# Attention scores in tiles of 32 queries instead of 64, and a split of the last activation and the last results over engines

## The chip, the cores and the metric

The kernel runs on one core of a Trainium2 chip. What counts is the time of one execution on the device, in microseconds (us); a kernel's time is the median of its runs. The core has a matrix engine (TensorE, PE in the profile, whose weight loads stand apart as PEld), VectorE (DVE), ScalarE (ACT), GpSimd (POOL) and SyncE (SP), which issues most of the transfers. Each works through its own list of instructions in order, and semaphores make one wait for another.

## The reference

The first stage is attention over 4 batches, 8 heads, 768 positions and a head width of 64, in which a query sees the keys at distance 0 to 127 behind it and the first 4 keys of the sequence (sinks). The second stage takes the 3072 x 512 result through a two-layer network with an activation of its own.

```
scores = scale * np.matmul(q, k.transpose(0, 1, 3, 2))
keep = (pos[None, :] < n_sink) | ((rel >= 0) & (rel < window))     # rel = query position - key position
a = softmax(np.where(keep, scores, -1e9));  attn = np.matmul(a, v)
x = attn with the 8 heads side by side, 3072 x 512
h = x @ w_in                                                       # 512 x 2048
sp = np.maximum(h, 0.0) + np.log1p(np.exp(-np.abs(h)))
out = (h * erf(sp)) @ w_out                                        # 2048 x 512
```

## The kernel before

**Attention.** It goes in 48 steps. A step `s` is a block of 256 queries (`g`, 12 blocks, 3 in each batch) for one pair of heads (`c`, 4 pairs). `score` (line 387) makes the scores of a step. The two heads of the pair, `h`, lie in the two halves of 64 partitions of the operand `kq` and write to two banks of PSUM, the halves of the tile `both` (`ps` in the profile). The 256 queries are two blocks `i` of 128. For each of them and each head there are two matmuls with 64 queries as the stationary operand: queries 0 to 63 (`lo`) against 208 keys, and queries 64 to 127 (`hi`) against 224 keys, which end in the 16 columns of the sinks. The blocks at the start of a batch (`gb == 0`) have no keys behind their first 128 queries, and there both matmuls of `i = 0` take 144. So a step has 8 matmuls, and since they are in plain float32, each shows as two records on PE: 16 records `L419`, over four quarters of the array (two halves of its rows by two halves of its columns).

A query needs only 128 of those keys. The kernel stores the scores of one query row by key position modulo 128: VectorE copies the wanted part of the overhanging columns onto the unwanted part with `copy_predicated` (line 432, the fold), under the mask `tri`. It takes two calls, one for the partitions of `lo` and one for those of `hi`. Then come the mask and the row minimum (L437), the exponential on ScalarE (L441), the sums and scaling (`norm`), a transpose (`ptrans`, through DRAM from step 15 on), the copies of halves on GpSimd (`phalf`, L528 and L537), and the product with the values (`av`, L579).

**Network.** `hidden` (L784, L788) multiplies a block with 128 columns of `w_in`, `act` (line 793) works out the activation of two such pieces at once, and `project` (L833 to L835) multiplies it with `w_out`. From block 2 on the operands are split into a high part and a low part in float32r: VectorE casts the high part `gh` (L817) and GpSimd subtracts to get the low part `gl` (L818). L833 and L834 need `gh`, and L835 needs `gl`. After the 16th piece of a block, `result` copies its two accumulators of 128 x 512 out of PSUM on ScalarE (L839, tile `ot`), and SyncE writes each to DRAM (L750).

**What sets the order.** The loop over `m` near line 730 emits for each sixteenth of a block its hidden matmuls, the attention work that `plan` puts there, the projections and the activation. `at(a, what)` gives each a priority, and the framework's scheduler makes each engine's final order from priorities and its own model of durations. The model's times are in that order, so an instruction of another size can move its neighbours.

Of the kernel before, what the change touches and what calls it, by code (L numbers as in the profile page):

```python
# [8 lines left out]
F32 = mybir.dt.float32  # L9
# [4 lines left out]
ALU = mybir.AluOpType  # L14
# [4 lines left out]
P = 128  # L19
# [23 lines left out]
DT = 12  # L43

TT = 15

NSINK = 22

# [2 lines left out]
FH = 8  # L51
# [5 lines left out]
UB = 4  # L57
# [4 lines left out]
def kernel(  # L62
# [11 lines left out]
    nc = tc.nc  # L74
    B, H, S, D = q.shape
    NT, DM = out.shape
# [3 lines left out]
    NF = DF // P  # L80
    GT = 256
    GPB = S // GT
    NG = B * GPB
    NU = 4
    NSTEP = NG * NPAIR
    KB, S3 = P + SW, 6 * SW
# [53 lines left out]
    def fast_path():  # L140
        with ExitStack() as st:
# [45 lines left out]
            set_mask(mask0)  # L187
            set_mask(mask1)

            tri = pers.tile([P, 192], mybir.dt.int8, name="tri")[:, :64]  # L190
            nc.vector.tensor_scalar(tri[:64], rf[:64, :64], float(P), None, op0=ALU.is_ge)
            nc.vector.tensor_scalar(tri[64:], rf[64:, 64:128], float(P), None, op0=ALU.is_lt)

# [10 lines left out]
            xp, early = {}, {}  # L206

            stp = {}
            mark = {}
            first, turn = [], []  # L210

            HP = P // 2
# [170 lines left out]
            def score(s, prev):  # L383

                g, c = divmod(s, NPAIR)
                gb = g % GPB
                d = stp[s]
                d["sum"] = small.tile([P, 2, 2], F32, tag="sum", name=f"sum_{s}")
                d["neg"] = small.tile([P, 2, 2], F32, tag="neg", name=f"neg_{s}")

                ps, both = [], None
                for h in range(2):
                    nm = f"ps_{s}_{h}"
                    if s == 1:
                        ps.append(ps_h.tile([P, 2, GT], F32, tag="h", name=nm).rearrange("p a t -> p (a t)"))
                    elif s == 2:
                        ps.append(ps_o.tile([P, DM], F32, tag="o", name=nm))
                    else:
                        if both is None:
                            both = ps_s.tile([P, 2, 512], F32, tag="s", name=f"ps_{s}")  # L400
                        ps.append(both[:, h, :])


                dx = KB + 80
                X = [80, 80 + dx]
                warm(ps[0][:, X[1] : X[1] + P], 3 if s == 0 else 0)
                for i in range(2):
                    qt = kq[:, c, 3 + i, :]
                    kt = kq[:, c].rearrange("p n t -> p (n t)")
                    runs = ((lo, KB * i, KB + 64, X[i]), (hi, KB * i + 64, KB + 80, X[i] - 80))  # L410
                    if gb + i == 0:
                        runs = ((lo, KB, KB, X[i]), (hi, KB, KB, X[i]))
                    for hf, r0, n, x in runs:
                        for h in (1, 0):
                            r = slice(64 * h, 64 * h + 64)
                            with at(pos(s), "rest") if s >= TT + AL else nullcontext():
                                prev = follow(
                                    prev,
                                    nc.tensor.matmul(ps[h][hf, x : x + n], qt[r, hf], kt[r, r0 : r0 + n], start=True, stop=True),  # L419
                                )  # L420

                i0 = int(gb == 0)
                for hf, x, y in ((lo, X[0], X[0] + KB), (hi, X[0] + 64, X[0] - 80)):
                    for t in (both,) if both is not None else ps:
                        t = t if both is not None else t.rearrange("p (h t) -> p h t", h=1)
                        n = t.shape[1]
                        o, w = (
                            t[hf, :, z : z + 2 * dx].rearrange("p h (i t) -> p h i t", i=2)[:, :, i0:, e : e + 64]
                            for z, e in ((min(x, 64), x - min(x, 64)), (min(y, 64), y - min(y, 64)))
                        )  # L430
                        mk = tri[hf].rearrange("p (a b t) -> p a b t", a=1, b=1).broadcast_to([64, n, 2 - i0, 64])
                        nc.vector.copy_predicated(o, mk, w)
                for i in range(2):
                    mk = mask if gb > 0 else (mask0, mask1)[i]
                    for h in range(2):
                        y = pst[:, s % RING, i, h, :]
                        mark["t", s] = nc.vector.tensor_tensor_reduce(  # L437
                            out=y, in0=ps[h][:, X[i] : X[i] + KB], in1=mk, scale=-scale, scalar=3.0e38, op0=ALU.add, op1=ALU.min,
                            accum_out=d["neg"][:, i, h : h + 1],
                        )  # L440
                        mark["e", s] = nc.scalar.activation(  # L441
                            y, y, AF.Exp, bias=d["neg"][:, i, h : h + 1], scale=-1.0, accum_out=d["sum"][:, i, h : h + 1]
                        )
# [268 lines left out]
            gs = {}  # L712
# [17 lines left out]
            for m in range(-LEAD, NG * NF + LAG + 2):  # L730
                a = m + LEAD
                live = 0 <= m < NG * NF
                if live:
                    g, f = divmod(m, NF)
                    if f % 2 == 0:
                        hp = mlp.hid_tile(m)
                    if f > 0:
                        with at(a, "hid"):
                            ahead = mlp.hidden(hp, xp[g], f)
                attn(a)  # L740
                w = m - LAG
                if 0 <= w < NG * NF:
                    g2, f2 = divmod(w, NF)
                    with at(a, "proj"):
                        mlp.project(gs[w // 2], g2, f2, lambda ins: follow(ahead if live and f and g >= 2 else None, ins))
                    if f2 == NF - 1:
                        for i in range(2):
                            r0 = (g2 * 2 + i) * P
                            with at(a, "res"):
                                nc.sync.dma_start(out[r0 : r0 + P, :], mlp.result(g2, i))  # L750
                if live:
                    if f == 0:
                        with at(a, "hid"):
                            mlp.hidden(hp, xp[g], f)
                    if f % 2 == 1:
                        with at(a, "act"):
                            gs[m // 2] = mlp.act(hp, m, m < NF + FH)

                while wn < 32 and a >= 1 and (wn < (0, 0, 3, 5)[a - 1] if a < 5 else wn < 2 * a - 4 or need(order[wn]) <= m + W1):
                    with at(a, "wc"):  # L760
                        wconv(order[wn], wn)
                    wn += 1
                    with at(a, "wl"):
                        for n in order[wl : wn + WQ]:
                            wload(n)
                            wl += 1
                for n in split.get(m, ()):
                    with at(a, "ws"):
                        wsplit(n, m)

    class make_mlp:
# [18 lines left out]
                )  # L790
            return last

        def act(self, hp, m, whole=False):
            work = self.work
            h = hp.rearrange("p a t -> p (a t)")
            r = work.tile([P, 512], F32, tag="r", bufs=1, name=f"r_{m}")
            if whole:
                acc = work.tile([P, 2, 512], F32, tag="g", bufs=2, name=f"gf_{m}")[:, 0, :]
            else:
                acc = None  # L800
            nc.scalar.activation(r, h, AF.Tanh, bias=b_t, scale=0.5)  # L801
            nc.scalar.activation(r, r, AF.Square, bias=b_v, scale=-0.5)  # L802
            nc.scalar.activation(r, r, AF.Square, bias=b_r)  # L803
            for i in range(3):
                u = work.tile([P, 512], F32, tag="u", bufs=UB, name=f"u{i}_{m}")
                sq = nc.scalar.activation(u, r, AF.Square, bias=b_a[i], scale=CS)  # L806
                x = h if i == 0 else acc
                if acc is None:
                    acc = u
                pr = nc.vector.scalar_tensor_tensor(out=acc, in0=u, scalar=CC[i] * CS**2, in1=x, op0=ALU.add, op1=ALU.mult)  # L810
            if isinstance(m, int):
                self.mark[m // 2] = sq, pr
            if whole:
                return (acc,)
            gt = work.tile([P, 2, 512], F32R, tag="g", bufs=2, name=f"g_{m}")
            gh, gl = gt[:, 0, :], gt[:, 1, :]
            nc.vector.tensor_copy(gh, acc)  # L817
            nc.gpsimd.tensor_tensor(gl, acc, gh.bitcast(F32), op=ALU.subtract)  # L818
            return gh, gl

        def project(self, gt, g, f, behind=lambda ins: ins):
# [166 lines left out]
```

## Time and profile before

| | us |
|---|---|
| lowest and highest of three runs | 700.12 and 702.70 |
| median | 701.39 |
| the profiled execution, its own time | 699.65 |
| its span, from the first to the last record | 697.95 |
| PE busy in it | 677.9 |

The profile shows one execution. Its own time stands 1.74 us under the median of the three runs, and 1.7 us of it lie outside the span. Busy times of an engine count a stretch once, even where records overlap. A matmul record lasts longer than the engine needs before it takes the next one, so the price of a matmul on PE is read from the distance between starts, not from the mean duration.

### The profile page before, as it was taken

How to read it: one execution, taken by the hardware profiler on the slowest of the kernel's cores; microseconds unless marked ns; L12 is line 12 of the kernel's file. 1: busy time of each engine (PE TensorE's matmuls, PEld its weight loads, DVE VectorE, ACT ScalarE, POOL GpSimd, SP SyncE). 2: the span in 40 equal slices, each digit the busy share in tenths (PEclk: the TensorE clock that was granted, in tenths of full speed). 3: DMA queues.
4: the chain of work that ended last, by engine and by line, in shares of the span. 5: the costliest groups of instructions: out<-in, count | busy, mean ns of one | idle time of the engine just before them, and what ended most of it. 6: DMA issues, size and time to landing. Idle time of an engine off the chain costs nothing. (4 is left out here: it accounts for less than half of the span.)

```text
span 698.0 us, 16215 instructions
## 1 busy us (share of the span) xinstructions
PE 677.9 (97%) x5550; PEld 565.4 (81%) x5550; DVE 548.2 (79%) x1473; ACT 494.3 (71%) x1157; POOL 305.4 (44%) x501
## 2 busy tenths in 40 slices
PE   8889999999999999999999999999999999999996
PEld 5657656788888788898888898898888898889895
DVE  7999997778889888878698788688689688664352
ACT  4787668987984776686596686687586686686572
POOL 3422371135434564473555444555445444542221
PEclk9999999999999999999999999999999999999999
DMA  7999402103216655543453553553453453320000
GB/s 215 265 320 397 114 16 58 38 16 60 57 36 125 135 118 102 132 92 77 108 111 72 117 96 74 118 115 76 111 103 77 101 106 70 73 49 1 31 2 35
DMA packets 246858, 70.10 MB, mean 100 GB/s; under 512 B 214704, under 2 KB 238896, under 8 KB 246768
## 3 DMA queue, kind: packets, MB, share of 16 engines
q1 hardware_dynamic: 246208, 68.92, 42.2%
q8 instruction: 46, 0.75, 0.5%
q14 instruction: 44, 0.36, 0.2%
q10 hardware_dynamic: 560, 0.07, 0.1%
HBM read 50.27 MB, written 18.42 MB: 98 GB/s over the span
## 5 line engine op out<-in xcount | busy, mean ns | idle before, releaser
L788 PE MATMUL h<-xh,wt 128*128 128x256 f32 x1408 | 268.4, 282 | 1.5 <-DVE gf L810 1.3
L788 PEld LDWEIGHTS h<-xh,wt 128*128 128x128 f32 x1408 | 222.7, 188 | 15.5 <-issue 7.6
L788 PE MATMUL h<-xl,wt 128*128 128x256 f32 x704 | 196.5, 279 | 0.0
L818 POOL TENSOR_TENSOR g<-u,g 128x512 fp32r<-128x512 f32 x84 | 112.6, 1340 | 166.9 <-DVE g L817 151.2
L806 ACT ACTIVATE u<-r 128x512 f32<-128x512 f32 x288 | 162.9, 622 | 18.8 <-DVE gf L810 7.5
L810 DVE SCALAR_TENSOR_TENSOR u<-u,u 128x512 f32<-128x512 f32 x168 | 132.1, 786 | 13.1 <-ACT u L806 0.8
L788 PEld LDWEIGHTS h<-xl,wt 128*128 128x128 f32 x704 | 132.5, 188 | 4.5 <-issue 1.1
L833 PE MATMUL o<-wt,g 128*128 128x512 f32 x336 | 133.0, 396 | 0.8 <-DVE g L817 0.8
L834 PE MATMUL o<-wt,g 128*128 128x512 f32 x336 | 132.0, 393 | 0.0
L835 PE MATMUL o<-wt,g 128*128 128x512 f32 x336 | 130.7, 395 | 0.7 <-POOL g L818 0.5
L441 ACT ACTIVATE pst<-pst,neg 128x144 f32<-128x144 f32 x192 | 77.4, 404 | 64.0 <-DVE neg L437 63.4
L801 ACT ACTIVATE r<-h 128x512 f32<-128x512 f32 x96 | 57.1, 594 | 44.8 <-PE h L788 43.5
L810 DVE SCALAR_TENSOR_TENSOR u<-u,h 128x512 f32<-128x512 f32 x84 | 56.5, 672 | 39.3 <-ACT u L806 36.6
L537 POOL TENSOR_SCALAR_AFFINE_SELECT pz<-pa 64x256 f32<-64x256 f32 (+1 forms) x96 | 57.2, 596 | 55.5 <-ACT pa L499 54.5
L833 PEld LDWEIGHTS o<-wt,g 128*128 128x128 f32 x336 | 63.1, 188 | 14.5 <-ACT u L806 1.7
L835 PEld LDWEIGHTS o<-wt,g 128*128 128x128 f32 x336 | 62.7, 188 | 14.8 <-POOL g L818 1.4
L834 PEld LDWEIGHTS o<-wt,g 128*128 128x128 f32 x336 | 63.1, 188 | 9.7
L817 DVE CAST g<-u 128x512 fp32r<-128x512 f32 x84 | 36.4, 433 | 36.7 <-PE o L835 33.3
L802 ACT ACTIVATE r<-r 128x512 f32<-128x512 f32 x96 | 60.7, 632 | 2.5
L803 ACT ACTIVATE r<-r 128x512 f32<-128x512 f32 x96 | 60.6, 631 | 2.7
L528 POOL COPY pz<-pa 64x256 f32<-64x256 f32 x66 | 29.6, 448 | 66.8 <-DMA pa<-pd 66.0
L419 PE MATMUL ps<-kq 64*64 64x208 f32 (+2 forms) x768 | 49.2, 346 | 0.7 <-ACT kq L372 0.7
(105 smaller groups left out, 921.7 us busy)
## 6 DMA issues: line engine op xcount, KB each, us to landing
pd<-turn SPq DMA_DIRECT2D x33, 320.0 KB, 2.6
pa<-pd SPq DMA_DIRECT2D x132, 80.0 KB, 2.7
ws<-in_moe_w_in_dram SPq DMA_DIRECT2D x16, 512.0 KB, 7.3
ws<-in_moe_w_out_dram SPq DMA_DIRECT2D x16, 512.0 KB, 10.1
out_dram<-ot SPq DMA_DIRECT2D x24, 256.0 KB, 2.1
v<-in_v_dram SPq DMA_DIRECT2D x56, 96.0 KB, 2.5
kq<-in_k_dram SPq DMA_DIRECT2D x144, 32.0 KB, 2.0
kq<-in_q_dram SPq DMA_DIRECT2D x144, 32.0 KB, 2.2
```

What stands on the lines that cost most here:

```text
L441: mark["e", s] = nc.scalar.activation(y, y, AF.Exp, bias=d["neg"][:, i, h : h + 1], scale=-1.0, accum_out=d["sum"][:, i, h : h + 1])
L537: mark["half"] = nc.gpsimd.affine_select(out=out, in_=x, pattern=[[0, 2], [0, 2 - i0], [-sg, HP]], compare_op=op, fill=0.0, base=0, channe ...
L788: last = nc.tensor.matmul(o, wt[NC * j + c][:, p, fs], xt[e][:, c, :], start=(m == 0), stop=(m == len(ops) - 1))
L801: nc.scalar.activation(r, h, AF.Tanh, bias=b_t, scale=0.5)
L802: nc.scalar.activation(r, r, AF.Square, bias=b_v, scale=-0.5)
L803: nc.scalar.activation(r, r, AF.Square, bias=b_r)
L806: sq = nc.scalar.activation(u, r, AF.Square, bias=b_a[i], scale=CS)
L810: pr = nc.vector.scalar_tensor_tensor(out=acc, in0=u, scalar=CC[i] * CS**2, in1=x, op0=ALU.add, op1=ALU.mult)
L818: nc.gpsimd.tensor_tensor(gl, acc, gh.bitcast(F32), op=ALU.subtract)
L833: behind(nc.tensor.matmul(o, gh[:, ws], wt[16 + f][:, 0, :], start=(f == 0), stop=False))
L834: nc.tensor.matmul(o, gh[:, ws], wt[16 + f][:, 1, :], start=False, stop=False)
L835: nc.tensor.matmul(o, gl[:, ws], wt[16 + f][:, 0, :], start=False, stop=(f == NF - 1))
```

## The change

From step 16 on (`SQ = 16`) the scores are made with 32 queries as the stationary operand, so four matmuls stand where two stood, each against 176 keys (144 in the blocks without earlier keys). They write one tile of PSUM that stays allocated from step 16 to the end (`banks["s"]`). At step 16 the widths are 272, 240, 208 and 176, so that every column that is read later has been written once. With the new layout the fold is one call over all 128 partitions and 128 columns, under a mask `tri` of 128 x 128 that is one more instruction at the start; the old one is renamed `tri2`. The low part of the last activation alone is made by VectorE instead of GpSimd. The last two results are each copied in two halves of 256 columns, one by ScalarE and one by VectorE, and each half is written by a transfer of its own, from the queues of ScalarE and SyncE.

```
-            tri = pers.tile([P, 192], mybir.dt.int8, name="tri")[:, :64]
-            nc.vector.tensor_scalar(tri[:64], rf[:64, :64], float(P), None, op0=ALU.is_ge)
-            nc.vector.tensor_scalar(tri[64:], rf[64:, 64:128], float(P), None, op0=ALU.is_lt)
+            tri2 = ... the same two instructions ...
+            tri = pers.tile([P, P], mybir.dt.int8, name="tri")
+            nc.vector.tensor_scalar(tri, rf[:, :P], float(P), None, op0=ALU.is_ge)
...
-                        if both is None:
-                            both = ps_s.tile([P, 2, 512], F32, tag="s", name=f"ps_{s}")
+                        if s <= SQ and both is None:
+                            both = banks["s"] = ps_s.tile([P, 2, 512], F32, tag="s", name=f"ps_{s}")
+                        both = banks["s"]
...
-                X = [80, 80 + dx]
+                X = [0, 240] if s >= SQ else [80, 160 + KB]
...
                     runs = ((lo, KB * i, KB + 64, X[i]), (hi, KB * i + 64, KB + 80, X[i] - 80))
+                    if s >= SQ:
+                        runs = [(slice(j, j + 32), KB * i + j, max(KB + 32, (272 - j) * (s == SQ)), X[i] + j) for j in range(0, P, 32)]
                     if gb + i == 0:
-                        runs = ((lo, KB, KB, X[i]), (hi, KB, KB, X[i]))
+                        runs = [(r[0], KB, KB, X[i]) for r in runs]
...
-                for hf, x, y in ((lo, X[0], X[0] + KB), (hi, X[0] + 64, X[0] - 80)):
+                folds = (... the two of before with tri2 ...) if s < SQ else ((slice(0, P), tri, X[0], X[0] + KB),)
+                for hf, m, x, y in folds:
...
-                                nc.sync.dma_start(out[r0 : r0 + P, :], mlp.result(g2, i))
+                                if w < NG * NF - 1:
+                                    nc.sync.dma_start(out[r0 : r0 + P, :], mlp.result(g2, i))
+                                    continue
+                                acc, hc = mlp.acc.pop((g2, i)), DM // 2
+                                for c0, copy, dma in ((0, nc.scalar.copy, nc.scalar), (hc, nc.vector.tensor_copy, nc.sync)):
+                                    ot = work.tile([P, DM], F32, tag="u", bufs=UB, name=f"ot_{g2}_{i}_{c0}")[:, :hc]
+                                    copy(ot, acc[:, c0 : c0 + hc])
+                                    dma.dma_start(out[r0 : r0 + P, c0 : c0 + hc], ot)
...
-                            gs[m // 2] = mlp.act(hp, m, m < NF + FH)
+                            gs[m // 2] = mlp.act(hp, m, m < NF + FH, nc.vector if m == NG * NF - 1 else nc.gpsimd)
...
-            nc.gpsimd.tensor_tensor(gl, acc, gh.bitcast(F32), op=ALU.subtract)
+            (eng or nc.gpsimd).tensor_tensor(gl, acc, gh.bitcast(F32), op=ALU.subtract)
```

The first place is PE around the scores of step 32, before the change (a row is line, operation, output<-inputs, size of the output, and how many follow each other; `av_30` is the product with the values of step 30, `o_6` an accumulator of block 6).

```order
L579 MATMUL av_30_5523<-pa_30_5270,v_30_5000 64x128 x2
L579 MATMUL av_30_5523<-pa_30_5270,v_30_5000 64x64 x4
L579 MATMUL av_30_5523<-pz_30_5406,vz_131 64x64 x8
L419 MATMUL ps_32_5540<-kq_130 64x208 x2
L419 MATMUL ps_32_5540<-kq_130 64x224 x2
L419 MATMUL ps_32_5540<-kq_130 64x208 x2
L419 MATMUL ps_32_5540<-kq_130 64x224 x2
L833 MATMUL o_6_0_5277<-wt_16_2058,g_97_5131 128x512
```

The same place on PE with the change, where the tile keeps the name of step 16 and the lines have moved down by 7 to 16.

```order
L588 MATMUL av_30_5622<-pa_30_5363,v_30_5087 64x128 x2
L588 MATMUL av_30_5622<-pa_30_5363,v_30_5087 64x64 x4
L588 MATMUL av_30_5622<-pz_30_5505,vz_133 64x64 x8
L426 MATMUL ps_16_2566<-kq_132 32x176 x16
L849 MATMUL o_6_0_5370<-wt_16_2060,g_97_5218 128x512
```

Sixteen matmuls of 176 columns stand between the same neighbours where eight of 208 and 224 stood. Elsewhere from step 16 on the scheduler has also moved hidden matmuls and projections against each other by up to about a dozen places. How often PE goes from one shape of array to another is the same in both orders, 169 times.

The second place is the end of VectorE's list, before the change, with the semaphores that each row waits for (`u0_191` is the last activation, `g_191` its high part).

```order
L817 CAST g_189_9036<-u0_189_9027 128x512 [waits DVE_49,PE_49]
L810 SCALAR_TENSOR_TENSOR u0_191_9080<-u0_191_9080,h_190_9039 128x512 [waits Activation_49]
L810 SCALAR_TENSOR_TENSOR u0_191_9080<-u1_191_9083,u0_191_9080 128x512 [waits DVE_49,Activation_49]
L810 SCALAR_TENSOR_TENSOR u0_191_9080<-u2_191_9086,u0_191_9080 128x512 [waits DVE_49,Activation_49]
L817 CAST g_191_9089<-u0_191_9080 128x512 [waits DVE_49,PE_49]
```

The end of VectorE's list with the change (`o_11_0` and `o_11_1` are the last two accumulators, `ot_11_0_256` the upper half of the copy of the first).

```order
L826 SCALAR_TENSOR_TENSOR u0_191_9275<-u0_191_9275,h_190_9234 128x512 [waits Activation_49]
L826 SCALAR_TENSOR_TENSOR u0_191_9275<-u1_191_9278,u0_191_9275 128x512 [waits DVE_49,Activation_49]
L826 SCALAR_TENSOR_TENSOR u0_191_9275<-u2_191_9281,u0_191_9275 128x512 [waits DVE_49,Activation_49]
L833 CAST g_191_9284<-u0_191_9275 128x512 [waits DVE_49,PE_49]
L834 TENSOR_TENSOR g_191_9284<-u0_191_9275,g_191_9284 128x512 [waits DVE_49]
L765 COPY ot_11_0_256_9314<-o_11_0_8980 128x256 [waits Activation_49]
L765 COPY ot_11_1_256_9320<-o_11_1_8981 128x256 [waits DVE_49,Activation_49]
```

The subtraction has come over from GpSimd, and two half copies stand behind it. Each of them waits for a semaphore of ScalarE (Activation), at the value that ScalarE's own copy of the other half of the same accumulator sets.

The third place is the end of ScalarE's list before the change.

```order
L803 ACTIVATE r_191_9076<-r_191_9076 128x512 [waits Activation_49]
L806 ACTIVATE u0_191_9080<-r_191_9076 128x512 [waits Activation_49,Pool_49]
L806 ACTIVATE u1_191_9083<-r_191_9076 128x512 [waits DVE_49]
L806 ACTIVATE u2_191_9086<-r_191_9076 128x512 [waits DVE_49]
L839 COPY ot_11_0_9116<-o_11_0_8785 128x512 [waits PE_49,Pool_49]
L839 COPY ot_11_1_9119<-o_11_1_8786 128x512 [waits DVE_49,PE_49]
```

The end of ScalarE's list with the change.

```order
L822 ACTIVATE u1_191_9278<-r_191_9271 128x512 [waits DVE_49]
L822 ACTIVATE u2_191_9281<-r_191_9271 128x512 [waits DVE_49]
L765 COPY ot_11_0_0_9311<-o_11_0_8980 128x256 [waits PE_49,Pool_49]
L766 DMA out_0_dram<-ot_11_0_0_9311 128x256 [waits Activation_49]
L765 COPY ot_11_1_0_9317<-o_11_1_8981 128x256 [waits DVE_49,PE_49]
L766 DMA out_0_dram<-ot_11_1_0_9317 128x256 [waits DMAHW3_49,Activation_49]
```

The copies are half as wide, and ScalarE now issues a transfer after each, the first of them ahead of its second copy.

## Rows read from the trace of the kernel before

**Rows 1.** The page's first part: busy us, share, instructions of each engine.
```profile
PE 677.9 (97%) x5550; PEld 565.4 (81%) x5550; DVE 548.2 (79%) x1473; ACT 494.3 (71%) x1157; POOL 305.4 (44%) x501
```
**Rows 2.** Busy time by stretch: from:to, length, PE busy (records), PEclk, DMA share, GB/s.
```profile
206.00:240.00 34.00, 31.79 (x297) 1.00 0.60 122
240.00:640.00 400.00, 399.99 (x3462) 1.00 0.45 93
```
**Rows 3.** PE's waits, 200 to 245 us: waiter <- releaser: us, times, longest.
```profile
PE av L579 <- POOL pa L537: 1.7, 2, 1.6
```
**Rows 4.** PE's timeline around step 32: start, us, line, operands, records [idle before <-releaser].
```profile
398.76 0.99 PE L419 MATMUL ps<-kq 64*64 64x208 f32 x16
399.68 0.51 PE L833 MATMUL o<-wt,g 128*128 128x512 f32 x1
```
**Rows 5.** PE's timeline around step 36, the first of a batch.
```profile
452.04 0.85 PE L419 MATMUL ps<-kq 64*64 64x144 f32 x16
452.82 0.51 PE L833 MATMUL o<-wt,g 128*128 128x512 f32 x1
```
**Rows 6.** PE's timeline of step 32 in three narrow windows: the records then under way.
```profile
398.76 0.41 PE L419 MATMUL ps<-kq 64*64 64x208 f32 x3
...
398.99 0.76 PE L419 MATMUL ps<-kq 64*64 64x208 f32 x12
...
399.17 0.58 PE L419 MATMUL ps<-kq 64*64 64x208 f32 x8
```
**Rows 7.** PE's timeline, 53 to 57 us: float32 matmuls on the whole array.
```profile
53.42 3.94 PE L784 MATMUL h<-xf,wf 128*128 128x256 f32 x17
```
**Rows 8.** VectorE by line and form: count | busy us, mean ns | idle before.
```profile
L432 DVE COPY_PREDICATED ps<-tri,ps 64x256 f32<-64x256 int8 x64 | 27.6, 431 | 3.5 <-PE ps L419 1.2
L702 DVE TENSOR_TENSOR wt<-wf,wt 128x512 fp32r<-128x512 f32 x32 | 21.5, 711 | 0.8 <-ACT wt L701 0.7
L599 DVE TENSOR_TENSOR xl<-av,xh 128x256 fp32r<-128x256 f32 x44 | 18.3, 417 | 9.0 <-ACT xh L598 8.7
L432 DVE COPY_PREDICATED ps<-tri,ps 64x128 f32<-64x128 int8 x28 | 8.3, 297 | 0.9
```
**Rows 9.** VectorE's timeline at the start of the program.
```profile
3.64 0.19 DVE L192 TENSOR_SCALAR tri<-rf 64x64 int8<-64x64 f32 x1
5.03 0.17 DVE L107 CAST tiny<-tiny 128x4 f32<-128x4 int32 x1 [1.20 <-DMA tiny<-in_window_dram]
```
**Rows 10.** The timeline of the end, all engines but PEld.
```profile
688.88 0.43 DVE L817 CAST g<-u 128x512 fp32r<-128x512 f32 x1
...
689.45 1.28 POOL L818 TENSOR_TENSOR g<-u,g 128x512 fp32r<-128x512 f32 x1 [3.61 <-DVE g L817]
...
690.17 0.39 PE L834 MATMUL o<-wt,g 128*128 128x512 f32 x1
690.79 0.74 PE L835 MATMUL o<-wt,g 128*128 128x512 f32 x2 [0.23 <-POOLq L956]
...
692.31 1.22 ACT L839 COPY ot<-o 128x512 f32<-128x512 f32 x2 [4.81 <-PE o L835]
692.92 0.96 SPq L750 DMA_DIRECT2D out_dram<-ot  x2
```
**Rows 11.** ScalarE by line and form.
```profile
L598 ACT CAST xh<-av 128x256 fp32r<-128x256 f32 x44 | 16.0, 365 | 31.2 <-PE av L579 30.8
L839 ACT COPY ot<-o 128x512 f32<-128x512 f32 x24 | 14.1, 586 | 19.2 <-PE o L835 18.4
```
**Rows 12.** A transfer issued on ScalarE's queue, from the timeline of the start.
```profile
1.76 0.49 ACTq L105 DMA_DIRECT2D tiny<-in_window_dram  x1
```

**Rows 13.** Transfers, from the page: operands, queue, count, KB each, median us to landing.
```profile
out_dram<-ot SPq DMA_DIRECT2D x24, 256.0 KB, 2.1
kq<-in_k_dram SPq DMA_DIRECT2D x144, 32.0 KB, 2.0
```
**Rows 14.** The same for the transfers after 690 us.
```profile
out_dram<-ot SPq DMA_DIRECT2D x2, 256.0 KB, 2.3
```

More of the change, by code (lines that the diff above doesn't have):

```diff
@@ L45 @@
 TT = 15
+SQ = 16
 NSINK = 22
@@ L188, in fast_path @@
             set_mask(mask1)
-            tri = pers.tile([P, 192], mybir.dt.int8, name="tri")[:, :64]
-            nc.vector.tensor_scalar(tri[:64], rf[:64, :64], float(P), None, op0=ALU.is_ge)
-            nc.vector.tensor_scalar(tri[64:], rf[64:, 64:128], float(P), None, op0=ALU.is_lt)
+            tri2 = pers.tile([P, 64], mybir.dt.int8, name="tri2")
+            nc.vector.tensor_scalar(tri2[:64], rf[:64, :64], float(P), None, op0=ALU.is_ge)
+            nc.vector.tensor_scalar(tri2[64:], rf[64:, 64:128], float(P), None, op0=ALU.is_lt)
+            tri = pers.tile([P, P], mybir.dt.int8, name="tri")
+            nc.vector.tensor_scalar(tri, rf[:, :P], float(P), None, op0=ALU.is_ge)
             kq = pers.tile([P, NPAIR, 5, KB], F32, name="kq")
@@ L208, in fast_path @@
             stp = {}
-            mark = {}
+            mark, banks = {}, {}
             first, turn = [], []
@@ L398, in score @@
                     else:
-                        if both is None:
-                            both = ps_s.tile([P, 2, 512], F32, tag="s", name=f"ps_{s}")
+                        if s <= SQ and both is None:
+                            both = banks["s"] = ps_s.tile([P, 2, 512], F32, tag="s", name=f"ps_{s}")
+                        both = banks["s"]
                         ps.append(both[:, h, :])
-                dx = KB + 80
-                X = [80, 80 + dx]
+                X = [0, 240] if s >= SQ else [80, 160 + KB]
+                dx = X[1] - X[0]
                 warm(ps[0][:, X[1] : X[1] + P], 3 if s == 0 else 0)
@@ L422, in score @@
                 i0 = int(gb == 0)
-                for hf, x, y in ((lo, X[0], X[0] + KB), (hi, X[0] + 64, X[0] - 80)):
+                folds = ((lo, tri2, X[0], X[0] + KB), (hi, tri2, X[0] + 64, X[0] - 80)) if s < SQ else ((slice(0, P), tri, X[0], X[0] + KB),)
+                for hf, m, x, y in folds:
+                    w = m.shape[-1]
                     for t in (both,) if both is not None else ps:
@@ L426, in score @@
                         n = t.shape[1]
-                        o, w = (
-                            t[hf, :, z : z + 2 * dx].rearrange("p h (i t) -> p h i t", i=2)[:, :, i0:, e : e + 64]
-                            for z, e in ((min(x, 64), x - min(x, 64)), (min(y, 64), y - min(y, 64)))
-                        )
-                        mk = tri[hf].rearrange("p (a b t) -> p a b t", a=1, b=1).broadcast_to([64, n, 2 - i0, 64])
-                        nc.vector.copy_predicated(o, mk, w)
+                        o, e = (
+                            t[hf, :, z : z + 2 * dx].rearrange("p h (i t) -> p h i t", i=2)[:, :, i0:, v0 : v0 + w]
+                            for z, v0 in ((min(q0, 512 - 2 * dx), q0 - min(q0, 512 - 2 * dx)) for q0 in (x, y))
+                        )
+                        mk = m[hf].rearrange("p (a b t) -> p a b t", a=1, b=1)
+                        nc.vector.copy_predicated(o, mk.broadcast_to([mk.shape[0], n, 2 - i0, w]), e)
                 for i in range(2):
@@ L791, in hidden, with act @@
             return last
-        def act(self, hp, m, whole=False):
+        def act(self, hp, m, whole=False, eng=None):
             work = self.work
```

## The prediction

> **What bounds the kernel now.** I read the share of busy time first. PE is busy for 677.9 of the 698.0 us of the span, ahead of VectorE's 548 [rows 1]. By stretches, PE is never idle between 240 and 640 us: 399.99 of 400 us, at a granted clock of 1.00, which is 2.4 GHz [rows 2]. So there the time is what PE needs for its list, and work taken from PE's list comes off the end. In the 34 us before, from 206 to 240, which hold the first steps that the change touches, 2.2 us are idle [rows 2]; PE waits there for GpSimd's halves (L537), 1.6 us once [rows 3]. The other busy engines matter where PE waits for them, at that spot and at the end. At the end PE waits for the low part of the last activation, then come two copies and two writes [rows 10].
>
> **The score matmuls.** A step without special keys takes PE 0.92 us: its first record starts at 398.76 and the next matmul on the whole array at 399.68 [rows 4]. The 16 records are four to each quarter of the array, one behind the other; rows that caught the second and third of the four begin at 398.99 and 399.17, so the first took 0.23 us, the others about 0.18 [rows 6]. A step at the start of a batch takes 0.78 us, from 452.04 to 452.82 [rows 5]. It differs in two of the four records of the longest chain, which have 144 columns for 224. So 2 x 80 columns are worth 0.14 us, 0.88 ns each. On the whole array a float32 record of 256 columns takes (3.94 - 0.39)/16 = 0.22 us, 0.87 ns a column [rows 7]. A column thus costs about the same whether one matmul runs in the array or four beside each other; with the 0.18 us for 208 columns I take 0.85 ns.
>
> With the change the array works in eighths and each has again four records, of 176 columns. The longest chain of before has 224. A normal step loses 4 x 48 x 0.85 = 0.163 us. In the 8 steps at a batch's start (24 to 27, 36 to 39) two of the four stay at 144, so they lose 0.082 us. Step 16 has a chain of 272 columns and gains 0.163. There are 32 steps from 16 to 47: 23 normal ones x 0.163 = 3.75, 8 x 0.082 = 0.65, less 0.16, makes **4.2 us off PE**. Two small terms cancel. Eight chains start in turn where four did, and three records start within 0.015 us [rows 6], so the last starts 4 x 0.007 = 0.03 us later. The first weights are 32 columns for 64: the first record took 0.05 us more than the later ones [rows 6], of which half, 0.025, goes.
>
> No row shows eight chains at once, so 0.85 ns a column is not shown for them. The price of a normal step lies between 0.76 us (as above) and 1.36 us, if eight chains got through no faster than two fours in turn (4 x 176 x 0.85 = 0.60 us more). I take the low end, since going from one matmul in the array to four beside each other did not change the price of a column, and because the halves and quarters of the array are busy with separate keys already today.
>
> **The fold.** Two calls of 0.431 us become one. The two sizes, 128 and 256 elements a partition, took 0.297 and 0.431 us [rows 8], 1.05 ns an element; 512 would take 0.70. VectorE is freed of 0.16 us in a normal step, and as much in the others (2 x 0.297 for 0.431), 5 us in all, of which nothing counts while PE does not wait for it. The new mask is one instruction of about 0.2 us like its neighbours, in the 1.20 us that VectorE waits for a transfer [rows 9]; without that cover it would cost those 0.2.
>
> **The order.** From step 16 on hidden matmuls and projections stand in other places on PE, and the other engines' lists follow. The number of shape changes of the array is the same, so PE's own work is not touched. Waits can come or go. Those of before from 206 to 240 us are 2.2 us [rows 2], which bounds a gain; for a loss I take as much. I take 0, since between 240 and 640 PE waited for nothing [rows 2], and the fold leaves the other engines more room.
>
> **The low part.** VectorE's cast of the last high part ends at 689.31, GpSimd's subtraction at 690.73, and PE, done with the high part at 690.40 (690.17 and a pitch of 0.23), goes on at 690.79 [rows 10]. VectorE needs 0.71 us for such a subtraction [rows 8], so it would end near 690.05 and PE would not wait: **0.39 us off**, with 0.35 us to spare. Nothing is queued behind it but the half copies, which PE's end releases later.
>
> **The last copies.** They look parallel in the code, but in the order VectorE's half waits for ScalarE's. After the last matmul there stood 0.59 us of copy on ScalarE [rows 11]; now it is 0.37 for 256 columns [rows 11] and then VectorE's half, between 0.30 and 0.42 us from its operations out of PSUM on 128 and 256 elements [rows 8]: 0.77, which is 0.18 later. The issue of a transfer, 0.49 us on ScalarE's queue [rows 12], stands between its two copies: 0.37 + 0.49 passes the 0.63 us between the starts of the two copies of before (1.22 for both, less 0.59) [rows 10, 11] by up to 0.2. Against that, the last write is half as large. A write of 256 KB landed 2.1 us after its issue, the last two 2.3, a read of 32 KB 2.0 [rows 13, 14], so halving the last one gives 0 to 0.3. For copies and writes together that is between 0.3 less and 0.4 more; I take 0, near the middle. The Trainium skill gives the reason for the wait: its page PSUM — Partial Sum Buffer (PSUM bank collisions raise a hardware error) says that ScalarE and VectorE may not read one bank at a time, and 512 float32 fill one. By the code alone, with both halves at once, the last copy would end 0.2 us earlier than before instead of 0.18 later; no row of before shows such a pair.
>
> **Sum.** 4.2 + 0.4 = 4.6 us off. The profiled execution, 699.65, becomes 695.0; it stands 1.7 under the median, so the median becomes 701.4 - 4.6 = **696.8**.
>
> **Rivals.** *The keys are the limit (slower).* The chains of one head stream their keys from the same 64 partitions, two at a time today and four then, and if that saturates, four go at half speed. A normal step would take 1.36 for 0.92 us, a batch's first steps 0.78 + 2 x 0.15 + 2 x 0.12 - 0.08 = 1.24 for 0.78. 24 x 0.44 + 8 x 0.46 = 14.2 us more, less 0.4: 715. For it speaks that no row has four, against it that two cost no more than one [rows 5, 7]. It decides from where a record of 176 columns takes 224 x 0.85 = 0.19 us instead of 0.15, and slowed to that point the change ends near 701 without a gain. *Records cannot start fast enough (slower).* A step has 32 records for 16. Rows bound the distance of two starts between 0.007 us (three within 0.015 [rows 6]) and 0.04 (16 starts in the 0.78 us of a batch's first step, less some 0.2 for the last record [rows 5]). At 0.03 the last would start 0.93 us in and a step would take 1.17, 0.25 more in 32 steps: 701.4 + 8.0 - 0.4 = 709. It decides from 0.022, where a step takes 0.92 again; the first three records speak against it [rows 6]. The page TensorE: Matmul & The Clock Gate of the Trainium skill (Part 1, Wait — 56ns, not 53.3ns?) gives 0.025 as the floor; by it alone a step would take 1.02 and the kernel 704, and the row of three records does not agree with it. *The new order waits.* If 2 us or more come back as waits for GpSimd or VectorE, as at 236 us, the time is 699 to 701.
>
> **How the numbers follow.** Forecast 0.68, 696.8 (695 to 698.5). Keys at half speed 0.11, slowed to no gain 0.08, records 0.03, new waits 0.10. The range leaves out the half-speed and records cases and little below: 694.0 to 702.0. About 0.5% is what a measurement can tell from no change, that is below 697.9 or above 704.9. Of the forecast 0.60 of 0.68 lies below 697.9; the rest of it, the new waits and the slowed case are the same, together 0.26; half speed and records are slower, 0.14.
>
> **What would show it.** Right: a score step near 0.76 us from first record to the next matmul, 0.70 at a batch's start, 1.08 at step 16; no gap before the last L835; VectorE's fold near 0.70 us; PE still busy throughout from 240 us. Wrong: a step at 0.92 or above, rows of L426 that start more than 0.02 us apart within a group, new waits of PE in the hundreds of ns, or a longer way from the last matmul to the end of the span than before.

## The result, and the profile after

The changed kernel is slower: 706.86 us, the median of five runs (702.55 to 707.18), against 701.51 for the kernel before, a ratio of 1.0063 with an interval of 1.0039 to 1.0088. The forecast was 696.8, with a range of 694.0 to 702.0. The profiled execution took 702.55 us with a span of 700.9; it is the fastest of the five, so a second profile was taken (below).

Lines have moved down: L419 is L426 now, L579 is L588, L788 is L804, L833 to L835 are L849 to L851, L810 is L826, L806 is L822. PE's timeline of step 32, which answers to [rows 4]:

```profile
401.28 0.83 PE L426 MATMUL ps<-kq 64*32 64x176 f32 x32
402.04 0.51 PE L849 MATMUL o<-wt,g 128*128 128x512 f32 x1
```

The step takes 0.76 us instead of 0.92, as forecast. But PE is no longer busy throughout from 240 us on. The two stretches of [rows 2] after the change (length, PE busy, granted clock, DMA share, GB/s):

```profile
206.00:240.00 34.00, 31.96 (x310) 1.00 0.58 115
240.00:640.00 400.00, 396.07 (x3953) 1.00 0.45 94
```

PE's waits from 206 us to the end (waiter, releaser, us, times, longest):

```profile
PE av L588 <- POOL pa L546: 2.6, 6, 0.9
PE h L804 <- DVE u L826: 1.8, 2, 1.2
PE o L851 <- POOL g L834: 1.3, 2, 1.0
```

Before there was one wait of this kind that mattered [rows 3]. To see where the time is, I cut the span of each profiled execution by the starts of the matmuls: the time up to step 16, then from there on the distance from each matmul's start to the next, summed by kind, so that a wait goes to the matmul ahead of it, and what follows the end of the last matmul. All in us; own time is that of the profiled execution.

| kernel | own time | up to step 16 | scores | values | hidden and projections | after the last matmul |
|---|---|---|---|---|---|---|
| before | 699.65 | 206.98 | 28.29 | 34.15 | 423.10 | 5.05 |
| changed | 702.55 | 207.56 | 24.10 | 34.43 | 428.00 | 6.37 |
| changed, again | 705.81 | 207.04 | 24.10 | 34.34 | 431.79 | 6.45 |
| changed, old order | 698.26 | 207.18 | 24.10 | 34.26 | 423.93 | 6.55 |
| old order, old copies | 695.10 | 206.91 | 24.10 | 34.26 | 422.39 | 5.34 |
| before, new order | 714.21 | 206.88 | 28.29 | 34.34 | 437.40 | 5.21 |
| before, new order, no writes | 708.79 | 206.59 | 28.29 | 34.34 | 431.53 | 5.95 |
| changed, no writes | 704.34 | 209.38 | 24.10 | 34.42 | 427.15 | 7.18 |
| before, new tail | 701.62 | 206.73 | 28.30 | 34.26 | 423.55 | 6.36 |
| before, no writes | 701.27 | 208.05 | 28.29 | 34.17 | 422.69 | 5.98 |
| tiles of 32 from step 20 | 703.35 | 207.17 | 24.74 | 34.33 | 428.51 | 6.50 |
| tiles of 32 from step 32 | 705.29 | 206.88 | 26.33 | 34.26 | 429.59 | 6.12 |

The scores give the 4.19 us that were forecast. Hidden matmuls and projections, whose number and size have not changed, take 4.9 us more in one execution and 8.7 in the other, and the way from the last matmul to the end 1.3 to 1.4 more. So two things are to be explained.

### The profile page after: what moved, and what is told of

It reads as the page before. It is cut to its first block, busy times and chain, and to the rows that moved or that the text cites. A ratio compares the mean times of both kernels' runs of the same rounds, so it can differ in the third digit from the quotient of the medians.

```text
span 700.9 us, 17196 instructions
## 1 busy us (share of the span) xinstructions
PE 676.2 (96%) x6062; PEld 563.9 (80%) x6062; DVE 540.7 (77%) x1445; ACT 493.5 (70%) x1157; POOL 308.6 (44%) x500
## 4 chain that ended last, share of the span: by engine, by line
PE 70%; DVE 12%; DMA 5%; ACT 4%; SPq 3%; issue 3%; POOL 2%; DVEq 0%; POOLq 0%; ACTq 0%
PE h L804 29%; PE o L851 9%; PE o L849 8%; PE o L850 8%; PE av L588 5%; PE ps L426 4%; PE o L846 3%; DMA pa<-pd 2%; DVE wf L696 2%; DVE gf L826 2%; DVE wf L699 2%; ACT pst L450 1%; SPq L242 1%; DVE pst L465 1%; PE h L800 1%
## 5 line engine op out<-in xcount | busy, mean ns | idle before, releaser
L804 PE MATMUL h<-xh,wt 128*128 128x256 f32 x1408 | 270.4, 282 | 3.1 <-DVE u L826 1.8
L804 PEld LDWEIGHTS h<-xh,wt 128*128 128x128 f32 x1408 | 223.2, 188 | 18.2 <-issue 10.2
L804 PE MATMUL h<-xl,wt 128*128 128x256 f32 x704 | 196.5, 279 | 0.0
L822 ACT ACTIVATE u<-r 128x512 f32<-128x512 f32 x288 | 163.3, 623 | 25.1 <-DVE gf L826 7.5
L826 DVE SCALAR_TENSOR_TENSOR u<-u,u 128x512 f32<-128x512 f32 x168 | 136.2, 811 | 13.3 <-ACT u L822 2.6
L804 PEld LDWEIGHTS h<-xl,wt 128*128 128x128 f32 x704 | 132.5, 188 | 4.9 <-issue 1.2
L849 PE MATMUL o<-wt,g 128*128 128x512 f32 x336 | 133.2, 396 | 1.0 <-DVE g L833 0.9
L851 PE MATMUL o<-wt,g 128*128 128x512 f32 x336 | 129.9, 395 | 1.5 <-POOL g L834 1.5
L450 ACT ACTIVATE pst<-pst,neg 128x144 f32<-128x144 f32 x192 | 77.4, 405 | 64.4 <-DVE neg L446 64.3
L826 DVE SCALAR_TENSOR_TENSOR u<-u,h 128x512 f32<-128x512 f32 x84 | 56.7, 675 | 54.1 <-ACT u L822 50.3
L546 POOL TENSOR_SCALAR_AFFINE_SELECT pz<-pa 64x256 f32<-64x256 f32 (+1 forms) x96 | 59.6, 620 | 59.6 <-ACT pa L508 58.4
L851 PEld LDWEIGHTS o<-wt,g 128*128 128x128 f32 x336 | 62.5, 188 | 15.3 <-POOL g L834 2.8
L849 PEld LDWEIGHTS o<-wt,g 128*128 128x128 f32 x336 | 63.1, 188 | 14.3 <-ACT pst L450 1.1
L833 DVE CAST g<-u 128x512 fp32r<-128x512 f32 x84 | 37.0, 441 | 30.1 <-PE o L851 23.1
L465 DVE TENSOR_SCALAR pst<-pst,sum 128x128 f32<-128x128 f32 x168 | 48.4, 349 | 1.3
```

The source lines that it names most:

```text
L450: mark["e", s] = nc.scalar.activation(y, y, AF.Exp, bias=d["neg"][:, i, h : h + 1], scale=-1.0, accum_out=d["sum"][:, i, h : h + 1])
L546: mark["half"] = nc.gpsimd.affine_select(out=out, in_=x, pattern=[[0, 2], [0, 2 - i0], [-sg, HP]], compare_op=op, fill=0.0, base=0, channe ...
L804: last = nc.tensor.matmul(o, wt[NC * j + c][:, p, fs], xt[e][:, c, :], start=(m == 0), stop=(m == len(ops) - 1))
L849: behind(nc.tensor.matmul(o, gh[:, ws], wt[16 + f][:, 0, :], start=(f == 0), stop=False))
L851: nc.tensor.matmul(o, gl[:, ws], wt[16 + f][:, 0, :], start=False, stop=(f == NF - 1))
```

## The experiments

**The order apart from the tiles.** Two kernels exchange the order and, up to the last copies, nothing else. Each lists the instructions of all engines in the order that the other kernel has, and chains them with dependencies that order without a wait:

```
+    def pin():
+        by = {i.name: i for i in nc.cur_bb.bb.instructions}
...
+            for prev, n in zip(names, names[1:]):
+                tc.add_manual_dep(by[n], prev, mybir.DependencyInfo(NoSync, DATA), reason="order")
...
     fast_path()
+    pin()
```

> The changed kernel with the instructions of every engine kept in the order of the kernel before (order-only dependencies; tail as changed). Theory 'order': the waits between 206 and 640 us fall back to the 3 us of the kernel before, the 4.2 us of the score matmuls stay, the tail costs 1.3: 701.5 - 4.2 + 1.3 = 698.6, between 697.5 and 700, ratio about 0.996. Rival 'tiles': tiles of 32 queries cost their 5 us in waits in whatever order (the longer fold on VectorE, more matmuls to issue): 705 to 707, ratio 1.005 to 1.008.

Measured: 697.02 us, ratio 0.9939 (0.9918 to 0.9959), half a us under the range expected. PE is again busy nearly throughout:

```profile
240.00:640.00 400.00, 399.25 (x3928) 1.00 0.45 93
```

> The kernel before with the instructions of every engine kept in the order of the changed kernel; score tiles, masks and tail as before. Theory 'order': 5 us slower than before, 705.5 to 708, with TensorE waiting for VectorE and GpSimd at hidden and projection matmuls near 237, 262, 355 and 513 us. Rival 'tiles': as before, 700.5 to 702.5.

Measured: 714.08 us, ratio 1.0171 (1.0146 to 1.0196), 6 us over the range expected. PE's waits in it (lines as in the kernel before, 8 further down):

```profile
PE h L796 <- DVE u L818: 6.4, 5, 2.5
PE av L587 <- POOL pa L545: 2.2, 2, 1.6
```

The tiles are cleared: in the old order they bring what was forecast. The order costs 8.8 us with the new tiles (705.81 against 697.02) and 12.4 us with the old ones (714.1 against 701.7), for which it was not made. In the profile of the latter PE's granted clock also falls to 0.5 twice, behind waits of 2.25 and 2.5 us.

**A second profile of the changed kernel.**

> The changed kernel once more, to see how far one profiled execution of it stands from the median of its times (the first profile took 702.55 us, the median of five was 706.86). Theory 'order': the score matmuls save the predicted 4.2 us, and the new order of the other matmuls gives back over 5 us in waits for the GpSimd and VectorE work in front of them; the median is 705 to 708, and a profile of a longer execution shows longer waits of the same kind between 206 and 640 us. Rival 'clock': the longer executions differ by a stretch in which the granted clock of TensorE stands at 0.5 for several us in the middle of the kernel.

Measured: 705.81 us, ratio 1.0056 (1.0031 to 1.0081), and the profiled execution took just that. Both theories have a part in it:

```profile
PE h L804 <- DVE u L826: 3.4, 3, 2.5
PE av L588 <- POOL pa L546: 3.4, 4, 1.7
```

The wait of 2.5 us begins near 513.6 us. Followed back through the timelines (start, us, line, output<-inputs, count, idle before with its releaser), first ScalarE in this profile:

```profile
503.85 0.59 ACT L855 COPY ot<-o 128x512 f32<-128x512 f32 x1 [2.40 <-PE o L851]
...
505.08 1.15 ACT L822 ACTIVATE u<-r 128x512 f32<-128x512 f32 x2
...
509.07 0.63 ACT L822 ACTIVATE u<-r 128x512 f32<-128x512 f32 x1 [2.58 <-DMA out_dram<-ot]
...
511.30 0.61 ACT L819 ACTIVATE r<-r 128x512 f32<-128x512 f32 x1
...
512.62 0.40 ACT L450 ACTIVATE pst<-pst,neg 128x144 f32<-128x144 f32 x1
...
513.02 1.65 ACT L822 ACTIVATE u<-r 128x512 f32<-128x512 f32 x3
```

then VectorE:

```profile
513.14 0.17 DVE L457 TENSOR_SCALAR sum<-sum 128x4 f32<-128x4 f32 x1 [0.79 <-ACT pst L450]
...
513.56 1.86 DVE L465 TENSOR_SCALAR pst<-pst,sum 128x128 f32<-128x128 f32 x3
515.34 0.68 DVE L826 SCALAR_TENSOR_TENSOR u<-u,h 128x512 f32<-128x512 f32 x1
```

and PE:

```profile
516.16 0.55 PE L804 MATMUL h<-xh,wt 128*128 128x256 f32 x1 [2.55 <-DVE u L826]
```

The hidden matmuls need a PSUM bank `h` that VectorE still has to read at 515.34. That read, which combines `h` with the first `u` of 513.02, comes late for two reasons. First, the third `u` of the activation before (509.07) waited 2.58 us for a result's write to DRAM: the copies `ot` and the tiles `u` share four buffers (`tag="u"`, `UB = 4`), two results and two `u` fill them, and the third can only start when the first result has been written. Second, between it and the next three `u` stand four exponentials (L450) where the old order has one, and VectorE has the sums (L457), which wait for the exponentials, and three scalings (L465) ahead of the read. The first `u` of 513.02 was ready near 513.6, so at the end it is the scalings that hold the read. The wait for the write is not fixed by the order: in the first profile, with the same lists, it was 1.47 us here. The same place before the change, ScalarE and then VectorE:

```profile
502.50 1.27 ACT L839 COPY ot<-o 128x512 f32<-128x512 f32 x2 [0.83 <-PE o L835]
...
505.80 0.63 ACT L806 ACTIVATE u<-r 128x512 f32<-128x512 f32 x1 [0.72 <-DMA out_dram<-ot]
...
508.93 1.14 ACT L806 ACTIVATE u<-r 128x512 f32<-128x512 f32 x2
```

```profile
509.83 0.65 DVE L810 SCALAR_TENSOR_TENSOR u<-u,h 128x512 f32<-128x512 f32 x1
```

The wait for the write was there too, 0.72 us, and PE did not notice: from the first result copy to the read of `h` it is 7.3 us, against 11.5 in the new order. In all, ScalarE waited 3.7 us for such writes before and 7.9 now. The queue of SyncE has changed as well. Before, the results' writes were issued ahead of the 320 KB write of `pd`; now that one goes first:

```profile
503.17 1.00 SPq L750 DMA_DIRECT2D out_dram<-ot  x2
504.27 0.40 SPq L487 DMA_DIRECT2D pd<-turn  x1
```

```profile
504.12 0.38 SPq L496 DMA_DIRECT2D pd<-turn  x1
504.60 0.47 SPq L760 DMA_DIRECT2D out_dram<-ot  x1
```

The two result writes there landed 3.2 us after their issue before (median), and 4.2 now. That the other write in front makes the difference fits, but no run isolates it.

The long wait has a price of its own. PE's stretches behind it (busy, granted clock, DMA share, GB/s):

```profile
514.00:516.00 2.00, 0.00 (x0) 0.95 0.27 43
516.00:518.00 2.00, 1.84 (x8) 0.50 0.00 0
518.00:520.00 2.00, 2.00 (x14) 0.69 0.56 154
```

After 2.55 us without a matmul the clock goes to its lower level, 1.2 GHz, until about 519 us, which costs 1.84 x 0.50 + 2 x 0.31 = 1.5 us of PE's time. In the first profile the same wait was 1.16 us, the clock stayed at 1.00, and the execution took 3.3 us less. That accounts for most of the distance between the two executions (1.4 us of wait and 1.5 of clock).

**The writes.** Two kernels, each in the order of the changed kernel, leave out the writes of eleven of the twelve groups, and a third does the same in the old order.

```
-                                    nc.sync.dma_start(out[r0 : r0 + P, :], mlp.result(g2, i))
+                                    mlp.result(g2, i)
```

> The changed kernel in its own order, with the 22 writes of the results of the first eleven groups left out (the copies out of PSUM stay, these rows of the output are not written). In its trace ScalarE waits 7.4 us for result writes in front of the third activation of a step (they share four buffers). Theory 'write wait': these waits are what delays VectorE and then TensorE in the new order: without the writes ScalarE's waits on them are gone, TensorE's waits for VectorE (1.8 and 3.4 us in two profiles) too, and the median falls from 705.8 by 3 to 6 us, to 700 to 703, with runs closer together. Rival 'slack': the new order leaves too little time between producers and consumers whatever the writes do: 704.5 or more.

Measured: 701.60 us, ratio 1.0003 (0.9990 to 1.0017), with runs from 700.23 to 704.34. PE's waits (lines of the changed kernel, 8 further down):

```profile
PE av L596 <- POOL pa L554: 2.3, 5, 0.7
PE o L859 <- POOL g L842: 2.1, 3, 1.3
PE h L812 <- DVE u L834: 0.7, 2, 0.4
```

> The kernel before in the order of the changed one, with the 22 writes of the first eleven groups' results left out (those rows are not written). With them this order gave 714.1 us, ScalarE waiting 9.2 us for the writes and TensorE 6.4 us for VectorE at hidden matmuls. Theory 'write wait': the 6.4 us fall to under 2, the median to 707 to 711; what stays above 701.5 is waits for GpSimd and VectorE that the order has without the writes too. Rival 'slack alone': 712.5 or more.

Measured: 708.62 us, ratio 1.0108 (1.0078 to 1.0137). PE's waits for VectorE at hidden matmuls fell from 6.4 to 3.9 us, less than expected.

> The kernel before in its own order with the same 22 writes left out (those rows are not written). Its ScalarE waits 3.7 us for result writes, 8 times, and TensorE's waits show nothing of it. Theory 'write wait' with slack: the order of before hides these waits, 700.5 to 701.8, no change. Rival: the writes cost this kernel as much as the changed one, 697 to 699.

Measured: 702.99 us, ratio 1.0025 (1.0010 to 1.0039).

Each set against the kernel before of its own session (701.73, 701.41 or 700.99), the writes cost 3.9 us in the new order with the new tiles and 4.7 with the old, in the old order nothing: there the kernel even took 1.6 us more without them. In its profile about 1 us more stands up to step 16, which I can't explain, and 0.9 after the last matmul, where SyncE's first instruction behind the branch at the program's end (see the tail below) comes 3.0 us after it instead of 0.5. So by the medians the waits for writes are somewhat under half of the 8.8 us, and up to 5.5 if leaving the writes out costs 1.6 us in the new order too. The traces can't say it closer: the profile without writes is of the slowest of ten executions, with the clock at 0.5 near 101 us, ahead of all that was changed, and its hidden matmuls and projections take 427.15 us, for 428.00 and 431.79 with the writes and 423.93 in the old order. What stays without the writes are short waits for GpSimd and VectorE. The second reason above is of that kind, but no run isolates it.

**The copies moved out of the way.** The changed kernel's order with each group's two result copies behind the third `u` of the step.

> The changed kernel in its own order, except that the two result copies of each group stand behind the third activation of the step in ScalarE's order instead of ahead of the first, so that no activation takes a buffer that a write still reads. Theory 'write wait': 699 to 703. Rival 'bank': the result's PSUM banks come free 2 us later and the next projections wait for them instead: 705 or more, with TensorE waiting for the copies.

Measured: 714.77 us, ratio 1.0194 (1.0173 to 1.0216); the rival is right.

```profile
PE o L857 <- ACT ot L863: 7.9, 9, 1.8
```

The wait for writes fell to 0.9 us, but PE now waits for the two banks of the results. The copies stand between two pressures, and the place ahead of the `u` is the better one. Buffers of their own for the results, 4 KB a partition for the two, were not tried.

**Other draws of the order.** The changed kernel with `SQ = 20` and `SQ = 32`.

> The same from step 20 on (28 steps). The scores save about 3.6 us, the tail costs 1.4. Theory 'order': another draw behind step 20; the sum of hidden and projection matmuls' time from step 16 on lies anywhere between the 422 to 424 us of the old order and the 428 to 432 of the changed kernel's: 698 to 706. Rival 'tiles': seven eighths of the changed kernel's loss: 704.5 to 706.

Measured: 703.53 us, ratio 1.0042 (1.0023 to 1.0062).

> The changed kernel with score tiles of 32 queries from step 32 on only (16 steps rather than 32, the order left to the scheduler). The scores save about 2.2 us, the tail costs 1.4. Theory 'order': up to the first converted step the order is that of the kernel before, so up to there nothing is lost; behind it the order is drawn anew, and the loss there is that of another draw: 700 to 706. Rival 'tiles': a converted step costs its 5 us / 32 wherever it stands, so half of the loss: 703 to 704.

Measured: 705.88 us, ratio 1.0071 (1.0042 to 1.0101).

Half of the steps lose as much as all of them: 6.5 us in hidden matmuls and projections for 16 converted steps, 5.4 for 28. The rival's ranges are missed on both sides, below for 28 steps and above for 16; the ranges of the order were so wide that lying in them says little. The loss does not go with the number of tiles, and the chained kernels show what it goes with: the order that the scheduler happens to make.

**The tail.** The kernel before with the new tail alone:

> The kernel before with the changed tail alone (low part of the last activation by VectorE, last results copied in column halves by ScalarE and VectorE with a write each); its order up to the tail is that of before. Theory 'jump': the end comes 1.0 to 1.8 us after that of before, less 0.39 for the low part, because ScalarE and VectorE reach the branch at the program's end only after the last copies, and their first instruction behind it starts some 3.7 us later: 702.1 to 702.9 against 701.5. Rival 'writes': only the chain of four copies costs, 0.5 us, less 0.39: 701.4 to 701.8, no change.

Measured: 702.52 us, ratio 1.0009 (0.9991 to 1.0027). The median can't tell the two apart, the trace can: 6.36 us after the last matmul instead of 5.05. The end of the changed kernel, which answers to [rows 10]:

```profile
693.88 0.37 ACT L765 COPY ot<-o 128x256 f32<-128x256 f32 x1 [4.28 <-PE o L851]
...
694.08 0.40 PE L851 MATMUL o<-wt,g 128*128 128x512 f32 x1
...
694.74 0.37 ACT L765 COPY ot<-o 128x256 f32<-128x256 f32 x1 [0.49 <-DVE ot L765]
...
695.15 0.42 DVE L765 COPY ot<-o 128x256 f32<-128x256 f32 x1 [0.44 <-ACT ot L765]
```

The last matmul ends at 694.48 and the last half copy at 695.57, 1.09 us later, where before it was 0.63. The writes land no later for it: SyncE's wait for the last of them ends 2.86 us behind the last matmul (3.30 before). What holds the end are the sequencers, the part of each engine that runs through its list. Every engine runs through a branch at the program's end (L972; start of the first and of the last):

```profile
L972 DVEq COMPARE_BRANCH  x1: 72/72/72, 696.0 to 696.0; - x1
L972 ACTq COMPARE_BRANCH  x1: 54/54/54, 696.1 to 696.1; - x1
...
L972 ACTq EVENT_SEMAPHORE  x1: 17/17/17, 699.8 to 699.8; - x1
L972 DVEq EVENT_SEMAPHORE  x1: 21/21/21, 699.8 to 699.8; - x1
```

From the branch to the first instruction behind it ScalarE takes 3.7 us and VectorE 3.8, and the program ends only after that: SyncE, done with its own waits at 697.9, stands 1.95 us until VectorE's semaphore comes. Before, VectorE had done with it at 692.4 (its branch was at 689.5), and ScalarE's 2.7 us ended with the last write:

```profile
L956 ACTq COMPARE_BRANCH  x1: 50/50/50, 693.5 to 693.5; - x1
...
L956 ACTq EVENT_SEMAPHORE  x1: 17/17/17, 696.2 to 696.2; - x1
```

The next kernel holds VectorE back by one small instruction and leaves the copies as they were:

```
+                                if w == NG * NF - 1 and i == 1:
+                                    nc.vector.tensor_copy(flag[0:1, 0:1], ot[0:1, 0:1])
```

> The kernel before with one added instruction: after the last result's copy VectorE copies one element of it to a tile that nobody reads. The last results are copied and written as before. Theory 'jump': VectorE now reaches the branch at the program's end about 4 us later than in the kernel before, right after the copy, and its first instruction behind the branch comes 3 to 4 us after that; the time from the last matmul's end to the end of the program rises from 5.05 us to 5.9 to 6.6, with the writes landing at the same 3.3 us as before. Rival 'writes': the 1.4 us of the changed tail come from four half writes on two queues; then this kernel ends as before, 4.9 to 5.3 us.

Measured: 701.36 us, ratio 1.0006 (0.9991 to 1.0021), and 5.59 us after the last matmul, between the ranges of the two. The mechanism is there, VectorE comes last:

```profile
L959 ACTq EVENT_SEMAPHORE  x1: 17/17/17, 696.6 to 696.6; - x1
L959 DVEq EVENT_SEMAPHORE  x1: 21/21/21, 697.6 to 697.6; - x1
```

but each of the two takes 3.0 us from its branch here, with the branches 1 us apart, against 3.7 and 3.8 where both branch at once. The last kernel takes the tiles of 32 and the low part, keeps the old order and goes back to the old copies:

> Score tiles of 32 queries in the order of the kernel before, the low part of the last activation by VectorE, and the last results copied and written as before (whole, by ScalarE, writes from one queue). Theory 'jump': the time from the last matmul's end to the end of the program falls from 6.4 to 6.6 us to 5.1: 697.0 - 1.4 = 695.6, between 694.6 and 696.6. Rival: the halves and the wholes end alike, 696.8 to 697.5.

Measured: 696.48 us, ratio 0.9934 (0.9915 to 0.9952), with 5.34 us after the last matmul. It is faster than both kernels. Its median stands 0.5 us under that of the old order with the new copies, which the runs can't tell apart; the 1.2 us after the last matmul stand in the traces.

## Why the prediction was wrong, point by point

**Score matmuls: right.** 4.19 us for 4.2; a step takes 0.757, 0.704 at a batch's start and 1.04 at step 16, for 0.76, 0.70 and 1.08. In step 32 the eight records of a group start 0.007 us apart, and the groups 0.173, 0.150 and 0.149 us behind each other, so 176 columns cost 0.15 us, 0.85 ns each, with eight chains in the array. Neither of the two rivals on the array came true. The floor of 25 ns between two starts, from the Trainium skill (TensorE: Matmul & The Clock Gate, Part 1, Wait — 56ns, not 53.3ns?), does not hold between matmuls in different parts of the array: here it is 7.

**Fold and mask: right.** The fold took 0.687 us for 0.70. The way to step 16 varies by more between profiles of one kernel (207.04 and 207.56) than the mask could cost.

**Low part: right.** VectorE's subtraction ends at 692.12, and PE goes on at 692.48, one pitch behind the matmul ahead of it.

**Order: the step that failed.** I took 0, and bounded the loss by the 2.2 us of waits that were there before. Nothing ties the one to the other: measured, the new order costs 8.8 us. That PE waited for nothing between 240 and 640 us says that the old order had slack of zero or more at each place, not how much, and so not what another order may shift before PE notices. The trace had a sign of it: ScalarE's eight waits for writes, 3.7 us that PE did not feel, were a margin in use. The rival that named new waits had the mechanism, but 2 to 4 us for it instead of 5 to 9, and no clock. At a chance of 0.10 it was far too low for a kernel whose order a scheduler makes from its own model.

**Last copies: wrong, a term was missing.** Between 0.3 less and 0.4 more was forecast, 1.3 to 1.4 more it is. The copies' chain cost 0.46, and the writes won as much. The branch behind the last instruction of ScalarE and VectorE was in no term.

**Sum.** Tiles, low part and order taken as 0 made 696.8; with the order really kept it is 697.0 with the new tail and 696.5 with the old one. That the 697.0 lies so near is in part luck: with the tail's 1.3 us the sum is 698.1, and the profiled execution of that kernel took 698.26.

## What to carry to other kernels

A change of sizes in a kernel whose order a scheduler makes has two effects, and only one of them is in the sum: compare the two orders with the other half held, by chaining the instructions in a listed order, before judging either. A bottleneck engine that never waits says nothing about its margin; list the waits of the engines behind it, above all those for buffers that a transfer must first release. Before splitting the last work over engines, look at which engine still has its branch to the program's end ahead of it.

## What the hardware showed that was not expected

- From a branch at the end of the program to the first instruction behind it ScalarE took 2.7 us and VectorE 2.9 (before, with 4 us between their branches), 3.0 each with 1 us between them, and 3.7 and 3.8 when they branched together. SyncE took 0.5 us in these, but 2.9 to 3.7 in the three kernels that leave the writes out. The records of the branches last 0.05 to 0.07 us. The Trainium skill gives some 108 ns for a compare-and-branch (Advanced Engine Details and Errata, Control Flow Timing); the runs here show that what follows can cost thirty times as much. In the changed kernel four transfers on the instruction queues begin 1.0 us behind the branches and end by 698.2, and ScalarE and VectorE go on at 699.8: loading of instructions may have a part in it, which was not tried apart.
- After 2.55 us without a matmul TensorE's granted clock went to 0.50 until about 3 us into the next matmuls (1.5 us of its time); after 1.16 us it stayed at 1.00.
- Eight float32 matmuls of 64 rows and 32 columns in different parts of the array start 0.007 us apart and get on at 0.85 ns a column, as fast as four.
